# A fused attention and two-layer expert kernel on one core: cast and rest of a split issued one position apart, the output's low weights loaded by a transfer of their own, q and k loads spread over ten positions

## Chip, core and metric

The kernel runs on one core of one Trainium2 chip. The metric is the device time of one execution in microseconds (us). Before the change three runs gave 1924.92, 1928.77 and 1932.10 us; the median is 1928.77 us.

## What is computed

```
x   = softmax(q kT / 8) v            8 batches, 8 heads, 576 tokens, chunks of 64 tokens, head size 64
y1  = (silu(x  wg) * (x  wv)) wo     4608 tokens, 512 -> 1536 -> 512
xn  = y1 / sqrt(mean(y1^2) + 1e-6) * rms_g
out = (silu(xn wg2) * (xn wv2)) wo2  4608 tokens, 512 -> 1536 -> 512
```

Attention is local to a chunk of 64 tokens. The weights arrive as 64-bit floats; q, k and v as 32-bit floats.

## The kernel before, in words

**Numbers.** Every matrix product of the two layers is made of three matmuls: each operand is split into a high part (`hi`, a cast on ACT to the fp32r type) and a low part (the rest, a subtraction on DVE or POOL), and `mm3` (line 585) issues high x high, high x low and low x high. So a split is a chain: cast on ACT, subtraction on another engine, and often a store or a matmul behind it.

**First layer.** The first 3584 tokens go in 7 blocks of 512 (`j` = 0 to 6), each through 12 chunks of the hidden size (`f`), so 84 iterations (line 1346). PE's order in iteration n is: `emit_g` (12 matmuls), `emit_v` (12 matmuls), then `emit_y` of iteration n-1 (12 matmuls). The loop calls `run(0)` after `emit_g`, `run(1)` after `emit_v`, `run(2)` at the end: three **positions** an iteration, 36 a block. `put` hangs any other work on a position, and `spread` hands out a list of DMAs over several positions. Engines execute in program order, and all DMAs but a few at the very end are issued by one queue, SP's, also in program order.

**What hangs on positions.** In blocks 1 to 5: attention of the later tokens (tiles of 128 tokens, one each 6.75 positions, `score_at`): maximum and exponentials (`att_m`), the normalisation on POOL (`att_n`, line 480), DVE transposes (`att_td`, line 496), the DVE transposes of the next tile's q and k (`trans_att`, line 409); the loads of q, k and v by groups of five chunks of 64 tokens (`load_qk`, `load_v`, `issue`, line 398). A group inside one batch row needs 32 q and k transfers, a group over a batch's end 64. Then the second layer's weights: load (`load_w64`, line 109), two ACT steps (`rebase`), two DVE steps (`to_f32`), sums of blocks on POOL (`comb_add`), splits (`comb_split`, cast line 218, subtraction line 219, store line 220). Then sums of the first layer's own weights for its last 1024 tokens (`whole`, `first_add`, `first_keep`), at the places of `w1_at`. Then the root mean square of the block before (`rms_...`).

**Low weights.** The high parts of the first layer's weights stay in memory. The low parts don't fit: block 0 makes them (`to_lo`, line 164) and stores them to DRAM through the list `keep` (line 1288), and each later iteration loads its chunk (`load_lo`, line 184): one tile of 768 KB that holds the parts of gate, value and output, in three slots.

```
            if n + 2 < len(iters) and n + 2 >= NF:
                load_lo(*iters[n + 2])
...
            sg, product = emit_g(l, j, f)
            run(0)
...
            if prev is not None:
                emit_y(*prev)
```

The order of chunks turns round from block to block, so a block begins on the three chunks that the last one ended on and loads nine.

In block 0 `conv1` runs three times an iteration. Call c converts weight c, makes the low part of weight c-1 and issues the store of weight c-6; weights come in the order gate, value, output of each chunk.

**The rest.** From about 915 us the program works through six superblocks `s` of 7 products each (a Strassen form): superblock 0 is the first layer of the last 1024 tokens, 1 to 5 are the second layer. A superblock has 84 steps of 6 matmuls (gate and value), then 84 of 3 (output). Weights come through a ring of 16 slots (`load_ring`); in superblock 0 `ring_split` (lines 886 and 888) splits the sums of weights when they have landed. `late` and `norm` hang work on the steps of superblocks 0 and 1: the root mean square of block 6 and of the last 1024 tokens (`tail_...`), and the last four pairs of output weights (`late_o`).

Of the kernel before, what the change touches and what calls it, by code (L numbers as in the profile page):

```python
# [19 lines left out]
def tile_kernel(  # L20
# [19 lines left out]
    nc = tc.nc  # L40
# [129 lines left out]
    def slot(j, f):  # L170
        if f >= 3:
            return slot(j, f - 3)
        return f if j == 0 else slot(j - 1, NF - 1 - f)

    def low_of(l, j, f, nm):
        if j and f < 3:
            return low_of(l, j - 1, NF - 1 - f, nm)
        return wl_[l, j, f][:, "gvo".index(nm)]

    def load_lo(l, j, f):  # L180
        if f < 3:
            return
        t = wlo.tile([P, 3, KD * P], F32R, tag=f"l{slot(j, f)}", name=f"l_{l}_{j}_{f}")
        nc.sync.dma_start(out=t.bitcast(F32), in_=lo1_d[chunk(j, f)])
        wl_[l, j, f] = t

# [27 lines left out]
    def comb_split(nm, fp, k, w=None):  # L214
        t = comb[1, nm, fp][k]
        if w is None:
            w = cv.tile([P, 2, HK], F32R, tag="ws", bufs=4, name=f"ws{nm}{fp}_{k}")
        nc.scalar.copy(w[:, 0], t)
        nc.gpsimd.tensor_sub(w[:, 1], t, w[:, 0].bitcast(F32))
        nc.sync.dma_start(out=w2_d["gvo".index(nm), fp, :, k], in_=w.bitcast(F32))  # L220

    PLAIN = {"g": ((0, 0), (0, 1), (1, 1)), "v": ((0, 0), (0, 1), (1, 1)), "o": ((0, 0), (1, 0), (1, 1))}

    def whole(nm, j, p, side):
        f = 2 * p + side
        t = cv.tile([P, KD * P], F32, tag="wa", bufs=2, name=f"wa{nm}{f}")
# [446 lines left out]
    def rms_split(j):  # L673
        n = blocks[j][1]
        acc = rms[j]
        ah = st.tile([P, 512], F32R, tag="ah", name=f"ah{j}")
        al = st.tile([P, 512], F32R, tag="al", name=f"al{j}")
        nc.scalar.copy(ah[:, :n], acc[:, :n])
# [25 lines left out]

    def rms_newton(j):
        n = blocks[j][1]
        ms, r = rms[j]
        nc.gpsimd.tensor_mul(ms[:, :n], ms[:, :n], r[:, :n])
# [43 lines left out]
    for i in range(NW // P, NT_):  # L752
        j = order[i] * P // NW
        if i >= 8:
# [24 lines left out]
        for c in (2 * i, 2 * i + 1):  # L779
            g = where[c][0]  # L780
            if g > 0 and c == groups[g][-1] and g + 2 < len(groups):
                dq, dv, nq = {4: (21, 18, 10), 7: (3, 9, 12), 8: (8, 12, 12)}.get(i, (1, 9, 7))
                spread(0, 0, b + dq, nq, lambda g=g: load_qk(g + 2))
                spread(0, 0, b + dv, 3, lambda g=g: load_v(g + 2))
    for j in range(1, NB):
        pj = j - 1
        for d in range(KD):
            put(0, j, 3 + 2 * d, lambda pj=pj, d=d: rms_sq(pj, d))
        put(0, j, 14, lambda pj=pj: rms_split(pj))
        put(0, j, 17, lambda pj=pj: rms_mm(pj))  # L790
        for z in range(4):
            put(0, j, (22, 22, 24, 24)[z] if j == 1 else (20, 21, 23, 26)[z], lambda pj=pj, z=z: rms_rec(pj, z))
        put(0, j, 29 if j == 1 else 27, lambda pj=pj: rms_newton(pj))
        for d in range(KD):
            put(0, j, (30, 32, 33, 34)[d] if j == 1 else 28 + 2 * d, lambda pj=pj, d=d: rms_x(pj, d))
# [4 lines left out]
    for x, (nm, f) in enumerate(w2):  # L800
        pos = NP + 6 * x
        put(0, 0, pos, lambda nm=nm, f=f: load_w64(1, nm, f))
        put(0, 0, pos + 4, lambda nm=nm, f=f: rebase(1, nm, f))
        put(0, 0, pos + 5, lambda nm=nm, f=f: to_f32(1, nm, f))
        if f >= NP2:
            fp = f - NP2
            for d, what in enumerate((
                ((comb_add, 3), (comb_add, 4)),
                ((comb_split, 3), (comb_add, 5)),
                ((comb_split, 4), (comb_add, 6)),  # L810
                ((comb_split, 0), (comb_split, 5)),
                ((comb_split, 1), (comb_split, 6)),
                ((comb_split, 2),),
            )):
# [62 lines left out]
    wsn = 0  # L877

    def ring_split(n):
        nonlocal wsn  # L880
        while wsn < min(n, wnext, len(wseq)):
            s, m, fp, k = wseq[wsn]
            wsn += 1
            if s == 0 and k > 2:
                t = wt[s, m, fp, k]
                nc.scalar.copy(t[:, 0], t[:, 1].bitcast(F32))
                eng = nc.gpsimd if wsn > 36 and m != "g" else nc.vector
                eng.tensor_sub(t[:, 1], t[:, 1].bitcast(F32), t[:, 0].bitcast(F32))
# [659 lines left out]
```

## Time and profile before

| what | value |
|---|---|
| median of three runs | 1928.77 us |
| the profiled execution | 1927.03 us, span from first to last instruction 1924.9 us |
| busy share | PE 92%, DVE 67%, ACT 42%, POOL 29% |
| mean granted TensorE clock | 0.967 of full speed |
| chain that ended last | PE 55%, DMA 13%, DVE 12%, POOL 7% |

"Busy" of PE counts a matmul from its issue to its modelled end, so that a row's count of matmuls against its length says more than its busy time. PEclk is the granted clock as a share of full speed (1.0 is 2.4 GHz, 0.5 is 1.2 GHz). A wait in the views is idle time of an engine and what ended it.

### The profile page before, as it was taken

How to read it: one execution, taken by the hardware profiler on the slowest of the kernel's cores; microseconds unless marked ns; L12 is line 12 of the kernel's file. 1: busy time of each engine (PE TensorE's matmuls, PEld its weight loads, DVE VectorE, ACT ScalarE, POOL GpSimd, SP SyncE). 2: the span in 40 equal slices, each digit the busy share in tenths (PEclk: the TensorE clock that was granted, in tenths of full speed). 3: DMA queues.
4: the chain of work that ended last, by engine and by line, in shares of the span. 5: the costliest groups of instructions: out<-in, count | busy, mean ns of one | idle time of the engine just before them, and what ended most of it. 6: DMA issues, size and time to landing. Idle time of an engine off the chain costs nothing.

```text
span 1924.9 us, 29765 instructions
## 1 busy us (share of the span) xinstructions
PE 1765.0 (92%) x9978; PEld 1468.4 (76%) x9978; DVE 1293.9 (67%) x2242; ACT 813.9 (42%) x1902; POOL 567.1 (29%) x551
## 2 busy tenths in 40 slices
PE   7989798888849979899988988999999999999998
PEld 5768576676638757788867776788888888999998
DVE  7976376575646666846768956795578458659566
ACT  7753333333324434323545633352345335336243
POOL 1003345255446345522244673021011001102000
PEclk9999899899979989999999999999999999999999
DMA  9976666677557567535465466868767776887986
GB/s 240 301 184 159 178 170 165 183 202 187 178 151 205 172 188 221 177 99 192 120 227 165 135 197 224 257 208 245 215 186 224 237 210 202 270 279 252 299 253 171
DMA packets 461670, 391.04 MB, mean 203 GB/s; under 512 B 278480, under 2 KB 334544, under 8 KB 461520
## 3 DMA queue, kind: packets, MB, share of 16 engines
q1 hardware_dynamic: 459920, 388.96, 68.9%
q8 instruction: 80, 1.31, 0.3%
q14 instruction: 70, 0.57, 0.1%
q10 hardware_dynamic: 1600, 0.20, 0.1%
HBM read 309.07 MB, written 79.95 MB: 202 GB/s over the span
## 4 chain that ended last, share of the span: by engine, by line
PE 55%; DMA 13%; DVE 12%; POOL 7%; issue 6%; SPq 4%; ACT 3%; DVEq 0%; POOLq 0%; ACTq 0%
DMA lo_scratch<-l 3%; SPq L398 3%; DVE pT L496 3%; PE v L586 2%; DMA l<-lo_scratch 1%; PE g L586 1%; PE v L588 1%; PE v L587 1%; PE g L588 1%; PE g L587 1%; ACT p L452 1%; PE ygA L587 1%; PE yvA L588 1%; PE ygA L588 1%; PE yvA L586 1%
## 5 line engine op out<-in xcount | busy, mean ns | idle before, releaser
L1028 POOL TENSOR_TENSOR h<-h,h 128x512 f32<-128x512 f32 (+1 forms) x36 | 47.3, 1313 | 558.4 <-DVE h L1006 539.4
L586 PE MATMUL g<-xh,wg 128*128 128x512 f32 x336 | 139.0, 414 | 36.1 <-DVE sg L599 34.3
L496 DVE STREAM_TRANSPOSE pT<-p 32x128 f32<-32x128 f32 x448 | 135.6, 303 | 46.5 <-POOL p L480 40.3
L1064 DVE TENSOR_TENSOR hp<-h,hp 128x512 fp32r<-128x512 f32 (+1 forms) x216 | 149.7, 722 | 6.2 <-ACT hp L1063 5.9
L588 PE MATMUL g<-xh,l 128*128 128x512 f32 x336 | 136.5, 406 | 15.1 <-DMA l<-lo_scratch 15.1
L1063 ACT CAST hp<-h 128x512 fp32r<-128x512 f32 (+1 forms) x216 | 122.0, 584 | 58.1 <-PE yvA L588 21.9
L986 ACT ACTIVATE sig<-sgt 128x512 f32<-128x512 f32 (+1 forms) x108 | 64.5, 597 | 185.7 <-DVE sgt L994 185.5
L586 PE MATMUL v<-xh,wv 128*128 128x512 f32 x336 | 134.8, 401 | 7.3 <-DVE sg L615 4.6
L587 PE MATMUL g<-xl,wg 128*128 128x512 f32 x336 | 135.4, 403 | 0.3 <-DVE xl L580 0.3
L987 DVE TENSOR_TENSOR sgt<-sgt,sig 128x512 f32<-128x512 f32 (+1 forms) x108 | 71.7, 664 | 93.8 <-ACT sig L986 93.7
L588 PE MATMUL v<-xh,l 128*128 128x512 f32 x336 | 131.8, 392 | 0.0
L587 PE MATMUL v<-xl,wv 128*128 128x512 f32 x336 | 131.5, 391 | 0.0
L925 POOL TENSOR_TENSOR xf<-xf,xf 128x512 f32<-128x512 f32 (+1 forms) x48 | 79.6, 1659 | 156.7 <-DMA wro<-w_scratch 67.8
L618 ACT CAST hh<-sg 128x512 fp32r<-128x512 f32 x84 | 51.8, 617 | 143.5 <-DVE sg L615 143.5
L586 PEld LDWEIGHTS g<-xh,wg 128*128 128x128 f32 x336 | 66.0, 196 | 55.4 <-DVE sg L599 39.4
L480 POOL TENSOR_TENSOR p<-p,r 128x512 f32<-128x512 f32 x36 | 39.7, 1102 | 225.2 <-DVE r L479 181.4
L599 DVE SCALAR_TENSOR_TENSOR sg<-sg,g 128x512 f32<-128x512 f32 x84 | 57.0, 679 | 61.4 <-ACT sg L598 60.9
L587 PE MATMUL y<-hl,wo 128*128 128x512 f32 x168 | 69.7, 415 | 28.6 <-DVE hl L620 28.2
L588 PEld LDWEIGHTS g<-xh,l 128*128 128x128 f32 x336 | 65.9, 196 | 32.1 <-DMA l<-lo_scratch 17.2
L586 PE MATMUL y<-hh,wo 128*128 128x512 f32 x168 | 69.0, 411 | 20.5 <-ACT hh L618 20.5
L598 ACT ACTIVATE sg<-g 128x512 f32<-128x512 f32 x84 | 50.0, 596 | 89.3 <-PE g L588 89.2
L586 PEld LDWEIGHTS v<-xh,wv 128*128 128x128 f32 x336 | 63.7, 190 | 24.0 <-DVE sg L615 7.2
(860 smaller groups left out, 5362.2 us busy)
## 6 DMA issues: line engine op xcount, KB each, us to landing
wrg<-w_scratch SPq DMA_DIRECT2D x210, 256.0 KB, 3.6
wrv<-w_scratch SPq DMA_DIRECT2D x210, 256.0 KB, 3.4
wro<-w_scratch SPq DMA_DIRECT2D x210, 256.0 KB, 3.2
l<-lo_scratch SPq DMA_DIRECT2D x54, 768.0 KB, 4.9
w_scratch<-wsg SPq DMA_DIRECT2D x42, 256.0 KB, 3.3
w_scratch<-wsv SPq DMA_DIRECT2D x42, 256.0 KB, 2.9
w64g<-in_moe_w_gate_dram SPq DMA_DIRECT2D x19, 512.0 KB, 6.3
w64v<-in_moe_w_val_dram SPq DMA_DIRECT2D x19, 512.0 KB, 5.4
```

What stands on the lines that cost most here:

```text
L398: nc.sync.dma_start(out=o, in_=i)
L496: nc.vector.transpose(out=pT[o:o + 32, :, r:r + 32], in_=pt[r:r + 32, :, z, b * 32:b * 32 + 32])
L586: nc.tensor.matmul(o, sh, mh, start=first, stop=False, skip_group_check=free)
L587: nc.tensor.matmul(o, sh, ml, start=False, stop=False, skip_group_check=free)
L588: nc.tensor.matmul(o, sl, mh, start=False, stop=last, skip_group_check=free)
L599: return sg, lambda: nc.vector.scalar_tensor_tensor(out=sg[:, :n], in0=sg[:, :n], scalar=1.0, in1=g[:, :n], op0=ALU.add, op1=ALU.mult)
L618: nc.scalar.copy(hh[:, :n], sg[:, :n])
L925: nc.gpsimd.tensor_sub(o, a, b)
L986: nc.scalar.activation(sg[:, :tw], src[:, :tw], AF.Sigmoid)
L987: nc.vector.tensor_mul(t[:, :tw], src[:, :tw], sg[:, :tw])
L1063: nc.scalar.copy(hh[:, :tw], src)
L1064: nc.vector.tensor_sub(hl[:, :tw], src, hh[:, :tw].bitcast(F32))
```

## The change

Nothing is computed otherwise. Slots and transfers of the low weights change; nearly all else is the order in which the same instructions are issued.

Low weights: gate and value in tiles of 512 KB with three slots (`load_lo`), output in tiles of 256 KB with two slots of its own (`load_lo_o`, called after `emit_y`). In block 0 the output's low part is made straight into such a slot.

```
-            wl_[0, 0, f] = wlo.tile([P, 3, KD * P], F32R, tag=f"l{f % 3}", name=f"l_0_0_{f}")
-        lo = wl_[0, 0, f][:, z]
+            wl_[0, 0, f] = wlo.tile([P, 2, KD * P], F32R, tag=f"l{f % 3}", name=f"l_0_0_{f}")
+        if z == 2:
+            wl_[0, 0, f, "o"] = wlo.tile([P, KD * P], F32R, tag=f"lo{f % 2}", name=f"lo_0_0_{f}")
+        lo = wl_[0, 0, f, "o"] if z == 2 else wl_[0, 0, f][:, z]
...
-        nc.sync.dma_start(out=t.bitcast(F32), in_=lo1_d[chunk(j, f)])
+        nc.sync.dma_start(out=t.bitcast(F32), in_=lo1_d[chunk(j, f), :, 0:2])
...
+    def load_lo_o(l, j, f):
+        if f < 2:
+            return
+        t = wlo.tile([P, KD * P], F32R, tag=f"lo{slot(j, f, 2)}", name=f"lo_{l}_{j}_{f}")
+        nc.sync.dma_start(out=t.bitcast(F32), in_=lo1_d[chunk(j, f), :, 2])
...
             if prev is not None:
                 emit_y(*prev)
+            if NF <= n + 1 < len(iters):
+                load_lo_o(*iters[n + 1])
             v_product()
```

Splits in two steps: `comb_split` becomes `comb_cast` and `comb_rest`, `rms_split` and `tail_split` give their cast to `rms_cast` and `tail_cast`, and POOL's product goes from `rms_newton` and `tail_newton` to `rms_mul` and `tail_mul`.

```
+    COMB = (
+        (7, comb_add, 3), (7, comb_add, 4), (8, comb_add, 5), (8, comb_cast, 3), (8, comb_cast, 4),
+        (9, comb_rest, 3), (9, comb_rest, 4), (10, comb_add, 6), (10, comb_cast, 0), (10, comb_cast, 5),
+        (11, comb_rest, 0), (11, comb_rest, 5), (12, comb_cast, 1), (12, comb_cast, 6),
+        (13, comb_rest, 1), (13, comb_rest, 6), (13, comb_cast, 2), (14, comb_rest, 2),
+    )
...
-        put(0, 0, pos, lambda nm=nm, f=f: load_w64(1, nm, f))
+        put(0, 0, pos + 1, lambda nm=nm, f=f: load_w64(1, nm, f))
         put(0, 0, pos + 4, lambda nm=nm, f=f: rebase(1, nm, f))
-        put(0, 0, pos + 5, lambda nm=nm, f=f: to_f32(1, nm, f))
+        put(0, 0, pos + 6, lambda nm=nm, f=f: to_f32(1, nm, f))
```

Attention and its loads (`a` is the tile's `score_at`; `b` is `a` - 1):

```
-            put(0, 0, a + 2, lambda i=i: att_n(i))
-            put(0, 0, a + 3, lambda i=i: att_td(i, 0))
-            put(0, 0, a + 4, lambda i=i: att_td(i, 1))
             if i + 1 < NT_:
-                put(0, 0, a + 5, lambda i=i: trans_att(i + 1))
+                put(0, 0, a + 2, lambda i=i: trans_att(i + 1))
+            put(0, 0, a + 3, lambda i=i: att_n(i))
+            put(0, 0, a + 4, lambda i=i: att_td(i, 0))
+            put(0, 0, a + 5, lambda i=i: att_td(i, 1))
...
-                dq, dv, nq = {4: (21, 18, 10), 7: (3, 9, 12), 8: (8, 12, 12)}.get(i, (1, 9, 7))
+                dq, dv, nq = {4: (21, 18, 10), 7: (3, 9, 12), 8: (8, 12, 12)}.get(i, (1, 11, 10))
                 spread(0, 0, b + dq, nq, lambda g=g: load_qk(g + 2))
-                spread(0, 0, b + dv, 3, lambda g=g: load_v(g + 2))
+                spread(0, 0, b + dv, 4, lambda g=g: load_v(g + 2))
```

The root mean square: cast at position 13, subtraction at 14, reciprocals at 20, 21, 23, 25, POOL's product at 26, Newton step at 28, scaling at 29, 31, 32, 34. `whole` gets a third buffer; `w1_at` puts 3, 4, 4, 4, 3 pairs into blocks 1 to 5 in place of 3, 3, 6, 3, 3, and output pairs run one iteration later.

The ring: casts two steps ahead of the subtractions, both further ahead than before, and POOL subtracts for the value weights alone.

```
-                eng = nc.gpsimd if wsn > 36 and m != "g" else nc.vector
...
+            while wsn[z] < min(n + 2 - 2 * z, wnext, len(wseq)):
...
+                    eng = nc.gpsimd if wsn[z] > 36 and m == "v" else nc.vector
...
-                    ring_split(wn + 5)
+                    ring_split(wn + 7)
...
-                ring_split(wn + 6)
+                ring_split(wn + 8)
```

`late_o` is drawn out from 12 to 19 steps (load at 0, first step at 4 in place of 3, casts and rests one step apart) and begins at steps 28 and 48 of superblock 0 and 24 and 42 of superblock 1, in place of 30, 50, 3 and 23; the tail's squares begin at step 0, its cast stands at 9 and 17, its subtraction at 11 and 19, its product at 37 and 45, its Newton step at 39 and 47.

## Rows read from the trace of the kernel before

**Rows 1.** The page's first part: busy us, share of the span, instructions.

```profile
PE 1765.0 (92%) x9978; PEld 1468.4 (76%) x9978; DVE 1293.9 (67%) x2242; ACT 813.9 (42%) x1902; POOL 567.1 (29%) x551
```

**Rows 2.** Windows, undisturbed: length; busy (count) PE, PEld, DVE, ACT, POOL; PEclk; DMA share; GB/s.

```profile
584.40:592.59 8.19, 8.19 (x37) 6.76 (x36) 6.18 (x18) 3.34 (x9) 6.73 (x10) 1.00 0.82 227
574.93:584.40 9.47, 9.47 (x101) 7.70 (x100) 6.17 (x10) 5.81 (x24) 3.29 (x5) 1.00 0.34 83
...
1250.00:1650.00 400.00, 400.00 (x1767) 331.02 (x1766) 285.21 (x427) 171.53 (x302) 55.99 (x37) 1.00 0.74 216
```

**Rows 3.** Windows, blocks 0 to 5 of the first layer.

```profile
25.03:151.40 126.37, 113.72 (x725) 89.38 (x726) 103.55 (x169) 84.17 (x149) 6.93 (x5) 0.97 0.88 244
151.40:284.47 133.07, 115.82 (x788) 91.78 (x786) 80.03 (x167) 48.63 (x167) 49.10 (x53) 0.92 0.62 167
284.47:417.45 132.98, 115.21 (x755) 90.35 (x754) 84.69 (x176) 49.00 (x158) 60.66 (x66) 0.94 0.65 178
417.45:574.93 157.48, 113.76 (x755) 89.82 (x754) 88.03 (x176) 50.53 (x160) 77.05 (x82) 0.88 0.63 178
574.93:701.29 126.36, 110.25 (x819) 88.14 (x818) 82.30 (x172) 52.02 (x176) 57.38 (x63) 0.95 0.69 193
701.29:814.92 113.63, 107.62 (x755) 85.67 (x754) 84.57 (x173) 47.93 (x156) 65.08 (x69) 1.00 0.63 188
```

**Rows 4.** Windows, the four stretches of blocks 1 to 4 that lose most.

```profile
195.70:233.80 38.10, 25.47 (x140) 18.80 (x138) 11.81 (x28) 11.09 (x31) 11.90 (x15) 0.78 0.63 173
334.60:368.50 33.90, 23.95 (x140) 18.03 (x139) 14.66 (x31) 10.58 (x21) 13.17 (x16) 0.80 0.67 185
514.80:574.93 60.13, 29.76 (x173) 23.74 (x172) 24.24 (x48) 11.28 (x35) 21.10 (x23) 0.74 0.55 153
665.20:690.90 25.70, 10.98 (x38) 7.92 (x37) 8.38 (x19) 6.22 (x25) 5.92 (x6) 0.73 0.72 210
```

**Rows 5.** PE's waits, 151.4 to 815 us: us in total, times, longest.

```profile
PE g L586 <- DVE sg L599: 28.4, 8, 14.7
...
PE g L588 <- DMA l<-lo_scratch: 15.1, 4, 5.2
```

**Rows 6.** Timeline of SP, ACT and DVE in the last stretch: start, length, instruction, idle before.

```profile
676.17 4.01 SPq L398 DMA_DIRECT2D xk<-in_k_dram  x8
...
682.50 0.40 ACT L218 CAST wsv<-wtv 128x256 fp32r<-128x256 f32 x1 [6.62 <-DMA w_scratch<-wsv]
...
684.05 1.21 DVE L135 SCALAR_TENSOR_TENSOR cmv<-w64v,cmv 128x512 uint32<-128x512 uint32 x1 [15.37 <-ACT cmv L125]
```

**Rows 7.** SP's own waits, blocks 1 to 4.

```profile
SPq L184 <- PE y_b L588: 63.3, 17, 10.3
```

**Rows 8.** Line 398 in blocks 1 to 4: issue time in ns, least, median, most.

```profile
L398 SPq DMA_DIRECT2D xq<-in_q_dram x209: 311/444/1236, 151.2 to 700.7; - x105
```

**Rows 9.** DVE's waits, 151.4 to 815 us.

```profile
DVE r L479 <- ACT r L456: 47.1, 22, 3.6
...
DVE pT L496 <- POOL p L480: 39.7, 16, 15.2
```

**Rows 10.** DVE's longest wait in block 0, 25 to 151.4 us.

```profile
DVE l L164 <- DMA lo_scratch<-l: 17.0, 6, 6.9
```

**Rows 11.** DMA issues of the page's kind: count, KB each, median us to landing.

```profile
lo_scratch<-l SPq DMA_DIRECT2D x36, 256.0 KB, 4.5
```

**Rows 12.** Timeline of DVE, block 0, the output's low part of chunk 10.

```profile
130.04 0.69 DVE L164 TENSOR_TENSOR l<-cro,wo 128x512 fp32r<-128x512 f32 x1
```

**Rows 13.** Timeline of SP, block 0, the 27th of 36 stores: output of chunk 8.

```profile
133.90 0.34 SPq L1288 DMA_DIRECT2D lo_scratch<-l  x1
```

**Rows 14.** Window, most of superblock 0 and the start of superblock 1.

```profile
960.00:1210.00 250.00, 220.51 (x894) 173.05 (x893) 180.20 (x246) 117.97 (x247) 127.93 (x117) 0.95 0.61 194
```

**Rows 15.** Groups by line and shape: busy us, mean ns, idle before.

```profile
L888 POOL TENSOR_TENSOR wro<-wro 128x256 fp32r<-128x256 f32 x24 | 24.6, 1047 | 5.4 <-ACT wro L886 5.3
...
L888 DVE TENSOR_TENSOR wrg<-wrg 128x256 fp32r<-128x256 f32 x24 | 15.3, 643 | 3.4 <-ACT wrg L886 3.4
```

More of the change, by code (lines that the diff above doesn't have):

```diff
@@ L225, in whole @@
         f = 2 * p + side
-        t = cv.tile([P, KD * P], F32, tag="wa", bufs=2, name=f"wa{nm}{f}")
+        t = cv.tile([P, KD * P], F32, tag="wa", bufs=3, name=f"wa{nm}{f}")
         h = whi[0, nm, f]
@@ L676, in rms_split @@
         ah = st.tile([P, 512], F32R, tag="ah", name=f"ah{j}")
+        nc.scalar.copy(ah[:, :n], acc[:, :n])
+        rms[j] = (acc, ah)
+    def rms_split(j):
+        n = blocks[j][1]
+        acc, ah = rms[j]
         al = st.tile([P, 512], F32R, tag="al", name=f"al{j}")
-        nc.scalar.copy(ah[:, :n], acc[:, :n])
         nc.gpsimd.tensor_sub(al[:, :n], acc[:, :n], ah[:, :n].bitcast(F32))
@@ L703, in rms_rec, with rms_mul @@
         nc.vector.reciprocal(out=r[:, a], in_=r[:, a])
+    def rms_mul(j):
+        n = blocks[j][1]
+        ms, r = rms[j]
+        nc.gpsimd.tensor_mul(ms[:, :n], ms[:, :n], r[:, :n])
     def rms_newton(j):
@@ L1148, in tail_split @@
         nc.scalar.copy(both[:, 0], acc)
+        tail[z] = (acc, both)
+    def tail_split(z):
+        acc, both = tail[z]
         nc.gpsimd.tensor_sub(both[:, 1], acc, both[:, 0].bitcast(F32))
@@ L1221, in late_o, with rest, cast @@
         spl = {"n": 0}
-        def split(k):
+        def rest(k):
+            comb_rest("o", fp, k)
+        def cast(k):
             n = spl["n"]
@@ L1412, in tile_kernel @@
         pj = NB - 1
-        late = {4 + 2 * d: [lambda d=d: rms_sq(pj, d)] for d in range(KD)}
-        late[14] = [lambda: rms_split(pj)]
-        late[17] = [lambda: rms_mm(pj, True)]
-        for z in range(4):
-            late[20 + 2 * z] = [lambda z=z: rms_rec(pj, z)]
-        late[28] = [lambda: rms_newton(pj)]
-        for d in range(KD):
-            late[30 + 2 * d] = [lambda d=d: rms_x(pj, d)]
-        norm = {}
-        for fp in range(LATE, NP2):
-            first, z = divmod(fp - LATE, 2)
-            for d, fn in enumerate(late_o(fp)):
-                (norm if first else late).setdefault((3 if first else 30) + 20 * z + d, []).append(fn)
+        late, norm = {}, {}
@@ new lines, in when @@
+        def when(t, n, fn, *a):
+            t.setdefault(n, []).append(lambda: fn(*a))
+        for d in range(KD):
+            when(late, 4 + 2 * d, rms_sq, pj, d)
+            when(late, 32 + 2 * d, rms_x, pj, d)
+            when(late, 20 + 2 * d, rms_rec, pj, d)
+        when(late, 13, rms_cast, pj)
+        when(late, 14, rms_split, pj)
+        when(late, 17, rms_mm, pj, True)
+        when(late, 28, rms_mul, pj)
+        when(late, 30, rms_newton, pj)
+        for fp, (t, n) in zip(range(LATE, NP2), ((late, 28), (late, 48), (norm, 24), (norm, 42))):
+            for d, fn in late_o(fp).items():
+                when(t, n + d, fn)
@@ L1434, in tile_kernel @@
-            norm.setdefault(34 + 8 * z, []).append(lambda z=z: tail_newton(z))
-            for d in range(KD):
-                norm.setdefault(37 + 2 * d + 8 * z, []).append(lambda z=z, d=d: tail_x(z, d))
+                when(norm, 2 * d + 8 * z, tail_sq, z, d)
+                when(norm, 29 + 2 * d + 8 * z, tail_rec, z, d)
+                when(norm, 41 + 2 * d + 8 * z, tail_x, z, d)
+            when(norm, 9 + 8 * z, tail_cast, z)
+            when(norm, 11 + 8 * z, tail_split, z)
+            when(norm, 16 + 8 * z, tail_mm, z)
@@ L1437, in tile_kernel @@
+            when(norm, 27, tail_sqrt, z)
+            when(norm, 37 + 8 * z, tail_mul, z)
+            when(norm, 39 + 8 * z, tail_newton, z)
         extra = {0: late, 1: norm}
```

121 lines of the change are left out of this document (58 added, 63 removed), and 8 rows, old and new, of the table w1_at.

## The prediction

> **What bounds the kernel now.** I began with the busy shares: PE is busy 92% of the span [rows 1], so a gain can only come from time in which PE idles or goes slowly. How much that is, the undisturbed stretches say [rows 2]: an iteration of the first layer takes 8.19 us, one with an attention tile 9.47 (1.28 more), and late in the run 1767 matmuls take 400 us, 0.2264 us each.
>
> Next the windows by block [rows 3]. A block should take 12 x 8.19 = 98.3 us and 1.28 for each of its 5, 5.5 or 6 tiles, so 104.7 to 106. Blocks 1 to 5 take 133.1, 133.0, 157.5, 126.4 and 113.6: 27.8, 28.3, 52.8, 20.4 and 8.9 us too much, 138 in all. Four short stretches hold most of it [rows 4]: against 18.1, 18.1, 25.9 and 8.2 us for their iterations they lose 20.0, 15.8, 34.2 and 17.5, together 87.5 us; 50.5 us are strewn over the rest. In these stretches the granted clock is 0.73 to 0.80: after PE has idled, part of the next matmuls run at 1.2 GHz in place of 2.4, and that is inside the 87.5. The other loss is at the seam of the layers: from 960 to 1210 us 894 matmuls stand where 250 / 0.2264 = 1104 would, so 47.5 us [rows 14].
>
> Then the reason. PE's rows name DVE's evacuation (28.4 us in 8 waits) [rows 5], but DVE is not the source. In the fourth stretch [rows 6] SP spends 4.01 us on eight k transfers; behind these stands the store of a finished weight; ACT waits 6.62 us for that store's buffer; DVE waits 15.37 us for ACT; PE waits for both. All four stretches lie where a group of q and k over a batch's end is loaded: 64 issues in seven positions. At 0.444 to 0.50 us each [rows 8, 6] that is 28 to 32 us of SP in 7 x 2.94 = 20.6 us (a position is a third of 8.83, the mean of the two iterations). And SP comes to it late: at each iteration's head it stops at the load of the low weights until PE has read the slot's output part, at that iteration's end, 63.3 us in 17 waits [rows 7]. Everything behind it is up to one iteration late.
>
> **The change part by part.**
>
> *Output's low weights apart.* The gate and value tile is free when PE has finished `emit_v` of the iteration before, so the load at the iteration's head no longer stops SP. The added wait is at `load_lo_o`, in position 2, for the same end of `emit_y` (up to 10.3 us each [rows 7]). Behind it stand only the DMAs of that position and of the next two; they go out when PE ends the iteration. SP is then late by a third of an iteration, some 3 us, in place of up to 9. The loads get more room: the 15.1 us that PE waited for them [rows 5] should go. Ten more issues a block at about 0.4 us cost SP 4 us a block.
>
> *q and k over ten positions.* 32 us of issues now fall in 29.4. With the other issues (some 10 in seven positions, 18 in ten, at 0.4 us) SP falls behind by 11.4 + 4 = 15 us before and 2.6 + 7 = 10 after; with the lateness at the start 24 and 13. The mean loss of the four stretches, 87.5 / 4 = 22, is 2 us less than the 24, so I take 2 us as the lateness that is borne: 11 us a stretch remain, 44, a gain of **43**. Bounds: the whole 87.5; or 25, if SP starts as late as now and 62 remain. I take the middle because both causes are halved, neither removed. The transposes of q and k come three positions earlier and their loads end three later: 15.5 - 9 = 6.5 positions or 19 us are left, and 13 us of lateness still fit; if not, DVE waits for them, 0 to 5 us a stretch, which the range carries.
>
> *Chains one position apart.* In blocks 1 to 5 DVE waits 47.1 us for the exponentials' sums, 39.7 for POOL's product [rows 9]; one position between each step hides 2.94 us, and the mean of the first is 2.1. The weight's load has a position less before its first step, but no longer waits behind the low weights. With block 3's six pairs cut to four, I take 30 of the strewn 50.5 us; bounds 10 and 45.
>
> *The seam.* The same cure for the root mean square, the tail and `late_o`, which in superblock 1 no longer starts together with the tail's squares. I take 18 of the 47.5; bounds 0 and 30. The 24 output subtractions that go from POOL to DVE cost DVE at most 24 x 0.643 = 15.4 us and relieve POOL of 24.6 [rows 15]. I price the swap at nothing, between 15 lost and 9 won, because DVE's part need not lie on PE's path. *Beside that:* the Trainium skill ("SBUF — State Buffer", Who interferes with whom) says that a VectorE instruction with two SBUF inputs and a GpSimd instruction that reads SBUF shut each other out for a whole instruction. By that, POOL's 24.6 us would come off DVE's waiting and the swap would win 24.6 - 15.4 = 9 us, the time 1839 us; by the rows alone it stays at 1848, and no row here separates the two.
>
> *Two output slots in block 0.* This one costs. Call c of `conv1` issues the store of weight c-6. Before, the wait for a slot was gate's: it needs a store issued two calls earlier, and DVE waited 17.0 us in 6 waits [rows 10]. Now the output part of chunk f needs that of chunk f-2 stored, issued one call earlier. A store lands 4.5 us after its issue [rows 11], a call comes each 126.37 / 36 = 3.5 us. In the trace the output part of chunk 10 was written at 130.04 us [rows 12], 3.9 us before the store of chunk 8's was even issued [rows 13]. So DVE will wait there in most of ten chunks. DVE is 103.55 of 126.37 us busy in this block [rows 3] and has little room; behind the waiting subtraction stand the next weight's conversion and the hidden layer's low part, for which PE waits. The landing less a call is 1 us, SP's own lateness adds 1 to 3: against 10 waits of 2 to 4 us stand the 17.0 us of gate's, most of which go. I take **12 us lost**; bounds 0 (the same stores only move the wait) and 28 (nothing is saved elsewhere).
>
> *At no cost:* the third `whole` buffer, the moved reciprocals, scalings and POOL products, and the ring's earlier casts, whose weights have 16 - 9 = 7 steps of 6 x 0.2264 = 1.36 us, 9.5 us, from issue; if that cover were gone, ACT would wait once a step.
>
> **The sum.** 43 + 30 + 18 - 12 = 79 us. The profiled execution took 1927.0 us (span 1924.9 and 2.1 around it), 1.7 below the median of 1928.8. 1927 - 79 = **1848 us**.
>
> **The rivals.** A difference within 0.5%, 9.6 us, can hardly be told from none here.
>
> *SP stays the bound (0.22).* The same q and k issues and 60 more; if the backlog and not the start decides, the stretches give back 25 only, the strewn waits 10, the seam 5, and block 0 takes 12 to 28: 12 to 28 us won, 1899 to 1915; I write 1900. For it: SP's 32 us in 29.4 leave it nothing spare.
>
> *Almost all goes (0.12).* The backlog stays under what is borne: 75 + 40 + 25 - 8 = 132, 1795. For it: the iterations between the third and the fourth stretch that I took as undisturbed lose nothing with the same work on all engines [rows 2].
>
> *No difference (0.08).* SP's halt at the low weights was idle time without consequence, and the waits moved with their steps: gains of about 20 meet block 0's loss, 1919 to 1937.
>
> *Slower (0.08): block 0's two slots.* Each late chunk delays DVE, DVE delays the conversion that frees SP's next load, SP issues the next store later: the waits feed one another. The price: at 7 us a chunk 70, less the 17 saved, 53 lost against gains of 35: 1945. It decides from about 6 us a chunk, if the stretches give no more than their lower bound. Against it: while DVE waits, SP works off its own queue, so that the next store comes sooner.
>
> **How the numbers follow.** My forecast has 0.50. Its own range is 1814 (the stretches give 65, half way to their bound, and block 0 takes nothing) to 1882 (they give 25 and block 0 takes 28). The range of 8 in 10 takes in the near part of "almost all" and SP's case: 1798 to 1910; outside lie 0.16 of the last two and some 0.04 below. Faster by over 0.5%: 0.50 + 0.22 + 0.12 = 0.84; within: 0.08; slower: 0.08.
>
> **What will show it.** Right: SP's wait of `load_lo` for `emit_y` gone, one of `load_lo_o` in its place; PE's wait for low weights gone; the four stretches still there but of about 11 us each; block 3 near 125 us; block 0 longer, at 138 us, with DVE's wait for stores at the output part and over 25 us; over 960 matmuls from 960 to 1210 us of the old place. Wrong: a block 0 that has not grown, four stretches as long as now, or a new wait of DVE for q and k.

## The result and the profile after

The changed kernel takes 1812.34 us, the median of four runs (1807.24 to 1814.78), against 1927.45 us for four runs of the kernel before beside it: a ratio of 0.9397, 95% interval 0.9369 to 0.9425, or 115 us. The forecast was 1848 us with a range of 1798 to 1910, so the direction and the range held, and the gain was 36 us larger than forecast. The profiled execution took 1807.24 us, 5.1 us less than the median; its span is 1805.5 us, at a mean granted clock of 0.990 (0.967 before).

The page's first part, engine by engine (PE was 92% busy before [rows 1]):

```profile
PE 1735.9 (96%) x9978; PEld 1455.5 (81%) x9978; DVE 1289.7 (71%) x2266; ACT 811.7 (45%) x1902; POOL 549.1 (30%) x527
```

PE issues the same 9978 matmuls in 29 us less of busy time (they run less often at the lower clock) and idles 90 us less. The 24 subtractions that went from POOL to DVE stand in the counts.

Windows by block, blocks 0 to 5, columns as in [rows 2]:

```profile
26.00:153.40 127.40, 113.95 (x724) 89.51 (x725) 101.90 (x169) 84.04 (x149) 5.26 (x4) 0.97 0.89 246
153.40:270.30 116.90, 111.06 (x788) 89.00 (x787) 80.87 (x169) 49.94 (x169) 49.87 (x53) 0.97 0.69 189
270.30:386.90 116.60, 109.10 (x756) 87.07 (x755) 81.97 (x171) 48.17 (x157) 68.76 (x74) 0.99 0.77 216
386.90:498.50 111.60, 107.12 (x755) 87.26 (x754) 82.55 (x175) 48.46 (x157) 65.96 (x71) 0.98 0.76 210
498.50:613.20 114.70, 109.78 (x819) 88.21 (x818) 85.62 (x177) 51.81 (x173) 65.87 (x70) 0.99 0.79 226
613.20:721.50 108.30, 106.46 (x755) 86.34 (x754) 81.88 (x174) 49.42 (x162) 61.80 (x67) 1.00 0.78 227
```

Beside [rows 3]: block 0 grew by 1.1 us; blocks 1 to 5 went from 663.5 to 568.1 us, 95.4 less. By the prediction's measure of undisturbed blocks they should take 525.4, so 42.7 us are still lost. Block 3, which lost most, gained most: 45.9 us.

Windows, the four stretches over a batch's end where they lie now, and last the seam, 93.5 us earlier than in [rows 14] because all that lies ahead of it is so much shorter:

```profile
206.40:239.20 32.80, 28.87 (x173) 21.91 (x171) 18.66 (x40) 13.34 (x35) 8.50 (x11) 0.95 0.79 241
305.40:361.10 55.70, 48.20 (x319) 37.04 (x312) 34.66 (x74) 24.54 (x80) 22.16 (x26) 0.97 0.78 224
483.70:529.90 46.20, 38.61 (x273) 30.04 (x272) 27.25 (x58) 15.54 (x53) 18.07 (x20) 0.96 0.74 198
599.70:634.10 34.40, 30.76 (x237) 23.37 (x236) 22.81 (x48) 12.84 (x39) 18.61 (x20) 0.95 0.74 199
866.50:1116.50 250.00, 235.87 (x1010) 188.92 (x1009) 202.04 (x297) 124.53 (x258) 110.44 (x94) 0.99 0.69 221
```

The stretches hold 3, 5, 4 and 3 iterations with 1, 2, 2 and 2 tiles, the second also two matmuls of the root mean square. At 8.19 us an iteration, 1.28 a tile and 0.2264 such a matmul they lose 7.0, 11.7, 10.9 and 7.3 us, 36.9 in all, in place of 87.5 [rows 4], so 5.8 of the 42.7 are strewn over the rest, in place of 50.5. At the seam 1010 matmuls stand where 894 stood and 1104 would: a loss of 94 x 0.2264 = 21.3 us in place of 47.5.

Waits of PE and SP in blocks 1 to 5, and two of DVE's (us in total, times, longest):

```profile
PE y L607 <- ACT hh L639: 11.7, 6, 4.1
...
PE g L609 <- DMA l<-lo_scratch: 1.2, 1, 1.2
...
SPq L193 <- PE y_b L609: 13.9, 12, 2.8
...
DVE hl L641 <- ACT hh L639: 87.2, 34, 10.7
...
DVE pT L517 <- POOL p L501: 4.3, 6, 2.1
```

and the first of DVE's two in the same blocks before:

```profile
DVE hl L620 <- ACT hh L618: 2.7, 5, 0.7
```

PE's wait for low weights fell from 15.1 to 1.2 us [rows 5]. SP's 63.3 us for `emit_y` in four blocks [rows 7] are 13.9 in five now, at `load_lo_o` (line 193), none over 2.8. DVE's wait for POOL's product went from 39.7 to 4.3 us, and its 47.1 us for the exponentials' sums [rows 9] no longer stand in the list. Not all of DVE's idle time went, though: it now stands 87.2 us at the low part of the hidden layer, for ACT's cast `hh`, where it stood 2.7 before. The largest wait that PE has left is for the same cast; what makes that late comes at the end of the experiments.

### The profile page after: what moved, and what is told of

It is laid out like the page before. It is cut to its first block, busy times and chain, and to the rows that moved or that the text cites. A ratio compares the mean times of both kernels' runs of the same rounds, so it can differ in the third digit from the quotient of the medians.

```text
span 1805.5 us, 29839 instructions
## 1 busy us (share of the span) xinstructions
PE 1735.9 (96%) x9978; PEld 1455.5 (81%) x9978; DVE 1289.7 (71%) x2266; ACT 811.7 (45%) x1902; POOL 549.1 (30%) x527
## 4 chain that ended last, share of the span: by engine, by line
PE 67%; DVE 11%; DMA 8%; SPq 4%; POOL 3%; ACT 3%; issue 3%; DVEq 0%; ACTq 0%; POOLq 0%
SPq L419 3%; PE v L607 3%; PE v L608 2%; PE v L609 2%; PE g L607 2%; PE g L608 2%; PE g L609 2%; DMA lo_scratch<-lo 2%; PE ygA L608 1%; PE ygA L609 1%; PE ygA L607 1%; PE y L607 1%; PE yvA L609 1%; PE yvA L608 1%; PE yvA L607 1%
## 5 line engine op out<-in xcount | busy, mean ns | idle before, releaser
L517 DVE STREAM_TRANSPOSE pT<-p 32x128 f32<-32x128 f32 x448 | 135.5, 303 | 10.6 <-POOL p L501 4.3
L641 DVE TENSOR_TENSOR hl<-sg,hh 128x512 fp32r<-128x512 f32 x84 | 72.5, 863 | 90.6 <-ACT hh L639 90.3
L607 PE MATMUL g<-xh,wg 128*128 128x512 f32 x336 | 133.1, 396 | 3.8 <-DVE sg L620 2.1
L609 PE MATMUL g<-xh,l 128*128 128x512 f32 x336 | 131.2, 390 | 1.2 <-DMA l<-lo_scratch 1.2
L608 PE MATMUL g<-xl,wg 128*128 128x512 f32 x336 | 131.1, 390 | 0.4 <-DVE xl L601 0.4
L609 PE MATMUL v<-xh,l 128*128 128x512 f32 x336 | 131.3, 391 | 0.0
L607 PE MATMUL y<-hh,wo 128*128 128x512 f32 x168 | 69.2, 412 | 11.7 <-ACT hh L639 11.7
L1032 DVE TENSOR_TENSOR h<-h,sgt 128x512 f32<-128x512 f32 (+1 forms) x108 | 74.0, 685 | 3.7
L607 PEld LDWEIGHTS v<-xh,wv 128*128 128x128 f32 x336 | 63.3, 188 | 16.4 <-ACT wo L156 2.2
```

The costliest lines, as they stand in the source:

```text
L517: nc.vector.transpose(out=pT[o:o + 32, :, r:r + 32], in_=pt[r:r + 32, :, z, b * 32:b * 32 + 32])
L607: nc.tensor.matmul(o, sh, mh, start=first, stop=False, skip_group_check=free)
L608: nc.tensor.matmul(o, sh, ml, start=False, stop=False, skip_group_check=free)
L609: nc.tensor.matmul(o, sl, mh, start=False, stop=last, skip_group_check=free)
L641: return product, lambda: nc.vector.tensor_sub(hl[:, :n], sg[:, :n], hh[:, :n].bitcast(F32))
L1032: nc.vector.tensor_mul(h[:, :tw], src[:, :tw], sgt[pos][:, :tw])
```

## The experiments

Twelve kernels ran, four runs each, beside six or seven runs of the kernel before on the same chip. Where time went inside a kernel is read between the first matmuls of its blocks; "seam" is the time of the 1600 matmuls from the last iteration of the first layer's loop on. All are in us (to 0.1), and each comes from one profiled execution, except for the median. The ratios are to the runs of the kernel before that stand beside each kernel.

| kernel | median | ratio to before, 95% | block 0 | blocks 1-5 | block 3 | seam |
|---|---|---|---|---|---|---|
| before | 1927.45 | | 126.4 | 663.5 | 157.5 | 411.4 |
| changed | 1812.34 | 0.9369-0.9425 | 127.5 | 568.1 | 111.6 | 385.3 |
| only_low | 1906.50 | 0.9880-0.9928 | 129.8 | 640.6 | 149.9 | 409.1 |
| only_qk | 1900.05 | 0.9857-0.9898 | 124.1 | 639.9 | 151.2 | 408.5 |
| only_chains | 1898.70 | 0.9851-0.9895 | 125.4 | 637.6 | 152.5 | 408.1 |
| only_seam | 1901.29 | 0.9860-0.9913 | 122.5 | 665.1 | 161.0 | 385.8 |
| no_qk | 1825.23 | 0.9461-0.9501 | 128.8 | 584.4 | 117.6 | 386.2 |
| no_chains | 1858.50 | 0.9633-0.9679 | 133.3 | 614.1 | 145.4 | 385.4 |
| no_w1 | 1816.48 | 0.9404-0.9453 | 131.2 | 573.2 | 111.7 | 386.9 |
| no_low | 1859.11 | 0.9637-0.9683 | 122.8 | 623.3 | 149.1 | 385.9 |
| wa_two | 1829.64 | 0.9469-0.9521 | 129.6 | 589.5 | 131.3 | 386.0 |
| low_wa3 | 1880.75 | 0.9742-0.9787 | 130.2 | 615.2 | 122.2 | 411.7 |
| slots_pool | 1815.16 | 0.9401-0.9446 | 122.2 | 577.4 | 108.7 | 390.4 |
| aligned | 1761.64 | 0.9124-0.9167 | 121.4 | 529.1 | 105.0 | 386.6 |

### Each part alone

Four kernels add one part to the kernel before. `only_low` has the two tiles of low weights and `load_lo_o`, with two buffers of `whole` as before. `only_qk` is two lines:

```
-                dq, dv, nq = {4: (21, 18, 10), 7: (3, 9, 12), 8: (8, 12, 12)}.get(i, (1, 9, 7))
+                dq, dv, nq = {4: (21, 18, 10), 7: (3, 9, 12), 8: (8, 12, 12)}.get(i, (1, 11, 10))
...
-                spread(0, 0, b + dv, 3, lambda g=g: load_v(g + 2))
+                spread(0, 0, b + dv, 4, lambda g=g: load_v(g + 2))
```

`only_chains` has the new places of the attention, of `COMB` and of the root mean square, with the old `w1_at`. `only_seam` has the ring, `late_o` and the tail.

> The kernel before with one part of the change: the output's low weights in tiles and transfers of their own. Theory A (SP's lateness is the source: its halt at the low weights and the bursts of q and k loads): SP starts each burst on time, the four stretches of blocks 1 to 4 lose some 55 to 60 us in place of 87, the rest a few less; about 1890 us. Theory C (the steps of the chains, issued too close, are the source; SP's lateness is borne): within 8 us of the kernel before, 1920 us or more. Block 0 shows the price of two output slots in either: 0 to 12 us.

> The kernel before with one part: q and k loads over ten positions, v over four. Theory A: the burst's own backlog falls from 15 to 10 us, the lateness at its start stays; each of the four stretches gains some 5 us: about 1907 us. Theory C: within 8 us of the kernel before.

> The kernel before with one part: in blocks 1 to 6 the steps of attention, of the second layer's weights and of the root mean square one position apart. Theory A: the strewn waits of blocks 1 to 5 go (30 of 50 us), the four stretches stay: about 1897 us. Theory C: the stretches go as well, 60 to 95 us in all: 1835 to 1867 us.

> The kernel before with one part: the ring's earlier casts, the output's subtractions on DVE, and the new places of late output weights and of the root mean square in superblocks 0 and 1. Both theories: blocks 0 to 6 as before, and the 26 us that the seam gave in the changed kernel: about 1901 us.

Against 1923.94 us for the kernel before, they gave 17.4, 23.9, 25.2 and 22.7 us. The seam came out as expected, and it is independent: 385.8 us, as in the whole change. `only_low` lies between the two expectations, `only_qk` gave 7 us more than theory A had, and `only_chains` lies where theory A had it. Of these three each gave something, and each left block 3 at 149.9 us or more. Together the four give 89 of 115 us. So either the parts help each other, or a part that was in none of them holds the missing 26.

### Each part taken back

Four kernels take one part out of the changed kernel: `no_qk` (the two lines above, reversed), `no_chains`, `no_w1` (the old `w1_at`) and `no_low`. `no_chains` and `no_low` also got the old list and two buffers, so each of them takes three things out at once. Of the lists the lines of block 3 are shown, new and old:

```
...
-        (3, 5, "g"), (3, 4, "o"), (3, 2, "v"), (3, 1, "v"),
...
+        (3, 0, "v"), (3, 1, "v"), (3, 2, "v"), (3, 3, "v"), (3, 4, "v"), (3, 5, "v"),
...
```

> The changed kernel, with q and k loaded over seven positions again. Alone this part gave 24 us, and the four parts tried alone give 89 of the 115 that the whole gives. Theory A (lateness of SP is what PE waits for, and a stretch is cured only when all the lateness in it falls under what the buffers bear): taking one cure away brings back more than it gave alone, 35 to 50 us, 1847 to 1862 us, and the four stretches again lose 10 to 20 us each. Rival B (the parts are independent, and the missing 26 us are the new places of the whole weights' pairs, which were in none of the four): 24 us, 1836. Rival C (the other cures leave SP enough room for the dense loading): under 10 us, 1820.

> The changed kernel, with the chains of the attention, of the second layer's weights and of the root mean square in their old places. Alone this part gave 25 us. Theory A: 35 to 50 us, 1847 to 1862 us, with DVE's waits for the exponentials' sums (10.6 us in the changed kernel, 46.5 before) back above 30. Rival B (independent): 25 us, 1837. Rival C (SP is what matters, and the chains only fill time in which PE waits for SP anyway): under 10 us, 1820.

> The changed kernel, with the whole weights' pairs of the second superblock in their old places (six in the last half of the blocks 3, three in blocks 1, 2, 4 and 5). Theory B (the parts are independent and this place list is the missing fifth): 26 us, 1838, most of it in block 3, which takes 130 us or more against 111.6. Theory A (the gains add up to more because the lateness is shared, and the pairs are one more share of it): 5 to 20 us, 1817 to 1832, block 3 at 115 to 125. Rival C (the list has no part in it): 1812, block 3 at 112.

> The changed kernel, with the low weights again in one transfer of three parts at the head of an iteration, and with that the old places of the whole weights' pairs and their two buffers, since the new places need the apart transfers. Alone the apart transfer gave 17 us. Theory A: 17 us and the pairs' share and more, 45 to 60 us, 1857 to 1872; SP waits again about 60 us for the output part's reader, and PE waits again some 15 us for the low weights. Rival B (independent parts): 17 us and what the run with the old places alone loses, some 43 at the most, 1829 to 1855. Rival C (with the other cures SP's halt at the head costs nothing): the loss of the run with the old places alone and under 8 us more.

`no_qk` lost 12.9 us, half of what the part gave alone, so theory A, by which taking one cure away costs more than it gave, failed there. `no_w1` lost 4.1, and the intervals of the two ratios overlap: the list isn't the missing part either. `no_chains` and `no_low` lost 46 and 47 and fitted A, but with block 3 back at 145 to 149, and the two share something else: two buffers of `whole`. One expectation of `no_low` failed: SP's wait for `emit_y` in blocks 1 to 5 came back (93.2 us in 24 waits), but PE waited only 2.5 us for low weights there, not 15, so it isn't the apart transfer alone that ended that wait. (DVE's wait for the exponentials' sums is back in `no_chains`, 48.3 us in 23 waits. The 10.6 and 46.5 us that its expectation puts beside it were the idle time ahead of DVE's transposes.) The timeline of `no_chains` shows what two buffers do. SP, POOL, DVE and PE in block 3, start, length, instruction, idle before:

```profile
517.83 1.56 POOL L273 TENSOR_TENSOR wav<-wav,wav 128x256 f32<-128x256 f32 x2
...
525.72 2.36 SPq L423 DMA_DIRECT2D xq<-in_q_dram  x5
528.13 0.43 SPq L423 DMA_DIRECT2D xk<-in_k_dram  x1
...
530.22 0.38 SPq L276 DMA_DIRECT2D w_scratch<-wav  x1
...
534.60 1.26 POOL L253 TENSOR_TENSOR wav<-wv,l 128x512 f32<-128x512 f32 x1 [15.21 <-DMA w_scratch<-wav]
...
536.50 1.04 POOL L505 TENSOR_TENSOR p<-p,r 128x512 f32<-128x512 f32 x1
...
537.58 2.51 DVE L521 STREAM_TRANSPOSE pT<-p 32x128 f32<-32x128 f32 x8 [16.38 <-POOL p L505]
...
542.43 0.80 PE L612 MATMUL y<-hl,wo 128*128 128x512 f32 x1 [14.46 <-DVE hl L645]
```

POOL finished the sums of a pair of whole weights at 519.4 us. The store of the half that goes out first was issued at 530.2: SP issued without a pause until then, 6.4 of the 10.8 us q and k. With two buffers POOL's next sum waited 15.2 us for that store, and behind it on POOL stood the attention's product, for which DVE waited 16.4 us; behind DVE's transposes stood the low part that PE needs, and PE waited 14.5. One late store of a weight that nobody needs yet stops three engines.

### The third buffer

`wa_two` is `no_w1` with one number changed; `low_wa3` is `only_low` with the opposite change.

```
-        t = cv.tile([P, KD * P], F32, tag="wa", bufs=3, name=f"wa{nm}{f}")
+        t = cv.tile([P, KD * P], F32, tag="wa", bufs=2, name=f"wa{nm}{f}")
```

> The kernel of the run no_w1 (the changed kernel with the whole weights' pairs in their old places, 1816) with two buffers for these weights in place of three. New theory D (the third buffer is the missing term: POOL waits for the store of the weight two before, 31 to 46 us in up to 8 waits in every run with two buffers and 0.7 to 8 in the runs with three, and behind POOL stand the attention's products, DVE and PE): 1840 to 1855 us, most of it in block 3 (130 to 145 us against 111.7), POOL's waits for these stores above 25 us. Theory A (the low weights and the chains each cost over 35 us to take away for their own sake): under 1822 us, block 3 below 116. If D holds, the low split and the chains are worth only the rest of 1859 and 1858 less this time.

> The kernel before, with the output's low weights apart (as in the run only_low, 1906.5 us) and a third buffer for the whole weights in the room that this frees; nothing else of the change. Theory D: POOL's waits for its stores fall from 34.7 us in 4 waits to under 10, and block 3 from 149.9 us to 125 to 135: 1882 to 1890 us. Theory A (the buffer counts only when all the other lateness is gone): within 5 us of only_low, 1902 to 1910.

`low_wa3` takes 1880.75 us, 25.8 less than `only_low` (the ratios' intervals are apart: 0.9742 to 0.9787 against 0.9880 to 0.9928), and block 3 falls from 149.9 to 122.2. The two ran beside different runs of the kernel before (1927.09 and 1923.94 us); by the gains over these, 46.3 and 17.4, the buffer is worth 28.9. That is the size of the missing 26: the five parts tried alone add up to 115 or 118 us, where the whole change gives 115.1 (the intervals leave each term some 5 us, and the parts overlap, as the next paragraphs show, so that the sum fits this well is chance). POOL's waits for these stores, first `only_low`, then `low_wa3`:

```profile
POOL wav L253 <- DMA w_scratch<-wav: 34.7, 4, 13.5
POOL wav L253 <- issue: 18.0, 3, 14.4
```

```profile
POOL wav L253 <- DMA w_scratch<-wav: 19.5, 4, 11.8
```

The wait halved rather than fell under 10, since SP's stores still come late there. In the other direction `wa_two` loses 13.2 us against `no_w1`, less than the 23 to 39 expected, with block 3 at 131.3 in place of 111.7 and POOL's wait up from 8.2 to 32.0, first `no_w1`, then `wa_two`:

```profile
POOL wav L249 <- DMA w_scratch<-wav: 8.2, 4, 3.1
```

```profile
POOL wav L249 <- DMA w_scratch<-wav: 32.0, 6, 9.8
```

So theory D holds, with a smaller price where the other cures are in. With `wa_two` as the base, which has the same list and buffers, the chains are worth 1858.5 - 1829.6 = 28.9 us and the apart transfer 1859.1 - 1829.6 = 29.5.

### Block 0's slots and POOL's subtractions

`slots_pool` is the changed kernel with a third slot for the output's low weights, two buffers of `whole` to make room for it, and the ring's subtractions for the output weights back on POOL:

```
-            wl_[0, 0, f, "o"] = wlo.tile([P, KD * P], F32R, tag=f"lo{f % 2}", name=f"lo_0_0_{f}")
+            wl_[0, 0, f, "o"] = wlo.tile([P, KD * P], F32R, tag=f"lo{f % 3}", name=f"lo_0_0_{f}")
...
-        t = wlo.tile([P, KD * P], F32R, tag=f"lo{slot(j, f, 2)}", name=f"lo_{l}_{j}_{f}")
+        t = wlo.tile([P, KD * P], F32R, tag=f"lo{slot(j, f, 3)}", name=f"lo_{l}_{j}_{f}")
...
-        t = cv.tile([P, KD * P], F32, tag="wa", bufs=3, name=f"wa{nm}{f}")
+        t = cv.tile([P, KD * P], F32, tag="wa", bufs=2, name=f"wa{nm}{f}")
...
-                    eng = nc.gpsimd if wsn[z] > 36 and m == "v" else nc.vector
+                    eng = nc.gpsimd if wsn[z] > 36 and m != "g" else nc.vector
```

> The changed kernel with two edits at places apart: three slots for the output's low parts in place of two (and, for the room, two whole buffers, with the new list of pairs), read in block 0; and the output parts' 24 subtractions of the ring back on POOL, read in the seam from block 6's end over 1600 matmuls. Block 0: if the two slots cost the 12 us forecast, 115 us in place of 127.5; if the store waits only moved from the gate part to the output part, as DVE's 14.1 us for stores in the changed kernel against 17.0 before say, 124 to 130 us. Seam: by the Trainium skill (SBUF - State Buffer, Who interferes with whom) POOL's subtractions would shut DVE out for 24.6 us and the seam gets some 9 us longer than 385.3; by the rows, which show no wait of PE for either, it stays within 3 us. Blocks 1 to 5: by theory D 15 to 30 us more than the 568 of the changed kernel; if the new list needs no third buffer, under 5.

Block 0 and the seam, windows of `slots_pool`, and under them DVE's wait for a store in its block 0:

```profile
25.50:147.70 122.20, 113.17 (x724) 89.66 (x725) 102.59 (x169) 83.78 (x149) 5.27 (x4) 0.96 0.87 243
817.60:1208.00 390.40, 372.67 (x1602) 300.42 (x1601) 318.16 (x435) 192.96 (x384) 161.59 (x138) 0.99 0.65 201
```

```profile
DVE l L166 <- DMA lo_scratch<-l: 6.8, 2, 3.7
```

A third slot took 5.3 us off block 0, neither the 12 forecast nor nothing. The table agrees on the size: block 0 takes 127.5 to 133.3 us in seven of the eight kernels with two output slots (mean 130.1), 122.2 to 126.4 in the six others (mean 123.9). The eighth, `aligned` at 121.4, also loads q and k otherwise. So the price is 5 to 6 us, and the two ranges don't meet.

The seam took 390.4 us, against 385.3 to 386.9 in the eight kernels that have the new ring and leave these subtractions to DVE (mean 386.0): 4.4 us more with POOL, in one trace. So the swap won some 4 us of the seam's 26. The reason stands in DVE's rows. The seam of the changed kernel, and two of DVE's groups in it, first in the changed kernel, then in `slots_pool`:

```profile
813.90:1199.20 385.30, 370.67 (x1601) 299.47 (x1601) 312.60 (x459) 192.81 (x384) 140.01 (x114) 1.00 0.66 204
```

```profile
L1090 DVE TENSOR_TENSOR hp<-h,hp 128x512 fp32r<-128x512 f32 x72 | 52.1, 752 | 1.0 <-ACT hp L1089 1.0
...
L1092 DVE TENSOR_TENSOR h<-t,h 128x512 f32<-128x512 f32 x12 | 8.2, 682 | 0.0
```

```profile
L1090 DVE TENSOR_TENSOR hp<-h,hp 128x512 fp32r<-128x512 f32 x72 | 58.1, 837 | 1.6 <-ACT hp L1089 1.6
...
L1092 DVE TENSOR_TENSOR h<-t,h 128x512 f32<-128x512 f32 x12 | 11.5, 954 | 0.0
```

With POOL subtracting, DVE has 24 instructions fewer and is busy 5.6 us longer, because the same instructions take longer. Of DVE's 128x512 subtractions in `slots_pool`'s seam (lines 947 and 1070 to 1094), the 92 with no POOL instruction beside them take 0.70 us at most, the 29 that overlap one of POOL's 24 subtractions 1.22 us at the median. The rule of the Trainium skill that the prediction cites ("SBUF — State Buffer", Who interferes with whom) has DVE and POOL shut each other out in such pairs: these rows agree with it. Of the 9 us that the prediction worked out by it, 4.4 came; that DVE's added time is what PE waited for isn't shown.

Blocks 1 to 5 lost 9.3 us with two buffers and the new list, between the two expectations. The third slot works there too (SP's wait of 13.9 us for `emit_y` is 1.0), so the 9.3 us are net of what that gave. So the new list and the third buffer cure the same thing: beside either one the other is worth 5 to 9 us, and without both blocks 1 to 5 take 21.4 us more (`wa_two`).

### Groups of q and k cut at the batches' ends

What is left in the changed kernel lies where a group spans two batches and needs two transfers for each tile. The chain in the third stretch is that of [rows 6], one link shorter: SP's store is late, ACT waits for the store's buffer, its cast `hh` stands behind that, and DVE and PE wait for the cast. SP, then ACT, DVE and PE of the changed kernel:

```profile
489.80 0.87 SPq L234 DMA_DIRECT2D w_scratch<-wsv  x2
...
492.49 0.40 ACT L228 CAST wsv<-crv 128x256 fp32r<-128x256 f32 x1 [8.86 <-DMA w_scratch<-wsv]
492.80 0.61 ACT L639 CAST hh<-sg 128x512 fp32r<-128x512 f32 x1
...
493.45 0.80 DVE L641 TENSOR_TENSOR hl<-sg,hh 128x512 fp32r<-128x512 f32 x1 [10.41 <-ACT hh L639]
493.47 0.50 PE L607 MATMUL y<-hh,wo 128*128 128x512 f32 x1 [4.14 <-ACT hh L639]
```

`aligned` cuts the groups at the ends, four or five chunks each, so that one transfer fills a tile:

```
-        groups.append(list(range(c0, min(c0 + 5, NCH))))
+        n = 4 if c0 % (2 * SC) == 0 else 5
+        groups.append(list(range(c0, min(c0 + n, (c0 // SC + 1) * SC))))
...
-                dq, dv, nq = {4: (21, 18, 10), 7: (3, 9, 12), 8: (8, 12, 12)}.get(i, (1, 11, 10))
+                dq, dv, nq = {4: (21, 18, 10), 7: (-1, 9, 10)}.get(i, (1, 11, 10))
```

> The changed kernel with the groups of q and k cut at the batches' ends, so that no group needs two transfers a tile: 416 issues in place of 544, at most 32 in ten positions. If the 37 us that the stretches over a batch's end still lose are SP's issues: 20 to 35 us less, 1777 to 1792 us, and these stretches under 3 us each. If they are the other work of these iterations (weights' chains on ACT, DVE and POOL): within 8 us of 1812, with the losses at the same iterations.

It takes 1761.64 us, 50.7 less than the changed kernel and more than expected (43.9 between the profiled executions, of which 39.0 in blocks 1 to 5 and 6.1 in block 0); the ratio to the kernel before is 0.9146 (0.9124 to 0.9167). Its blocks 1 to 5:

```profile
147.10:253.60 106.50, 106.21 (x788) 86.86 (x787) 80.88 (x168) 49.90 (x169) 50.55 (x53) 1.00 0.79 209
253.60:358.60 105.00, 105.00 (x755) 86.17 (x754) 82.39 (x170) 48.17 (x157) 68.78 (x74) 1.00 0.85 237
358.60:463.60 105.00, 105.00 (x755) 86.19 (x754) 87.21 (x179) 50.00 (x160) 66.28 (x71) 1.00 0.86 243
463.60:571.20 107.60, 106.67 (x819) 87.31 (x818) 85.80 (x170) 52.29 (x177) 65.26 (x70) 1.00 0.88 242
571.20:676.20 105.00, 105.00 (x755) 86.17 (x754) 81.18 (x172) 48.55 (x158) 61.49 (x67) 1.00 0.73 217
```

In three blocks PE never stops and the clock stays at 1.00; the 104.7 us that the prediction worked out for an undisturbed block are reached within 0.3. The same bytes of q and k go through in less time, and in the changed kernel's stretches the DMA engines were busy for a share of 0.74 to 0.79 (up to 0.88 here), so the stretches were not short of bandwidth: what they lacked was SP's time. This version beats both kernels. It also moves the loads of two groups (the list's special places), and block 0 took 121.4 us in it; which of the 6 us there are owed to that wasn't tried apart.

## Why the prediction was right, and where its terms were off

**What bounds the kernel.** Shown right for blocks 1 to 5, with one addition. PE's idle time there came from SP's lateness: SP's halt at the head, its bursts and what waited behind them each gave time when cured alone, and with half the issues in a burst next to nothing is left of it (PE's waits in these blocks are 100.3 us before, 24.4 in the changed kernel, 1.2 in `aligned`). SP's wait for `emit_y` in these blocks, before and in `only_low`:

```profile
SPq L184 <- PE y_b L588: 84.7, 24, 10.3
```

```profile
SPq L193 <- PE y_b L613: 23.5, 8, 8.3
```

The addition: `only_chains` gave 25.2 us with this wait at 90.1 us, so the chains were a source of their own.

**The stretches (43 forecast).** Measured 50.6. The reason was right: 36.9 us remain in four stretches where 44 were to remain. Taking the middle between the bounds was near. But undoing the spread costs only 12.9 us, so this term was not the spread's and the apart transfer's alone: the chains and the buffer took their part in block 3, where the third stretch lies (131.3 us in `wa_two`, 145.4 in `no_chains`, 111.7 in `no_w1`).

**The strewn waits (30 forecast, 45 the upper bound).** Measured 50.5 - 5.8 = 44.7. Here the prediction named a wrong cause for part of it. It set "the third `whole` buffer" under "at no cost" and credited the pairs of block 3 that were cut from six to four; the runs give 4 us for that list, where the buffer is in, and 13 to 29 for the buffer. Block 3, forecast near 125, took 111.6. The row that says so was in the trace of before, among POOL's waits in blocks 1 to 5, which the prediction did not read:

```profile
POOL wav L228 <- DMA w_scratch<-wav: 43.4, 5, 16.0
```

The prediction saw the last link of that chain, DVE's 39.7 us for POOL's product [rows 9], and put all of it down to a chain issued too close. That was some half of it: this wait is 23.7 us in `only_chains`, and the buffer alone takes it from 44.6 (`only_low`) to 25.2 us (`low_wa3`).

**The seam (18 forecast).** Measured 26, and 22.7 by `only_seam`. Within the bounds; the swap, priced at nothing, is 4 of it. Which of the rest is owed to the ring's earlier casts, to `late_o` and to the tail wasn't tried apart, so the cause given for this term is argued and not shown.

**Block 0 (12 lost).** Measured 1.1 in the two traces, 5 to 6 over all kernels: 1.1 is luck, the longest of the six blocks without the price beside the shortest of the seven with it. The wait came where it was foretold, at the output's low part, but in the changed kernel it is 14.1 us in 7 waits for stores, 2.0 each, not over 25; with the same slots `no_chains` has the most:

```profile
DVE lo L166 <- DMA lo_scratch<-lo: 14.1, 7, 3.6
DVE lo L166 <- PE v L609: 6.7, 1, 6.7
```

```profile
DVE lo L166 <- DMA lo_scratch<-lo: 23.8, 8, 7.4
```

The gate's 17.0 us [rows 10] went, and these came in their place: mostly the lower bound's reason, "the same stores only move the wait". The size was off, not the step from DVE's wait to PE's time, though "DVE has little room" was read off a busy share of 82%, without a row that shows PE waiting. DVE's idle time before its low parts, all reasons together, is 21.5 to 23.8 us in the seven kernels whose block 0 takes 127.5 us or more, and 6.8 to 17.0 in the seven where it takes 126.4 or less; `aligned`, with 14.2 us and two slots, is one of the latter. With two slots, then, the wait is some 7 us longer in the mean (22.3 us in the seven, 15.2 in the five kernels with one tile of low weights), and the block some 6.

**The sum.** 95.4 + 26.1 - 1.1 for block 0 and - 1.0 at the start and the end make the 119.4 us between the spans; the forecast was 79. Of the 40 between, 22 are blocks 1 to 5, 8 the seam, 11 block 0. The 1812 us lie just outside the forecast's own range (1814 to 1882), and nearer to the 1795 of "almost all goes" than to 1848. Of the rivals, "SP stays the bound" fell: the apart transfer and the spread did lower SP's lateness. "Almost all goes" came nearer than its chance of 0.12 said for the strewn waits and the seam, not for the stretches. The slower case fell with its mechanism: DVE's waits for stores at the output part are at most 3.6 us long in the changed kernel and 7.4 in any with two slots, and never more than 23.8 in all, where the case needed 6 to 7 a chunk in ten chunks.

## What to carry to other kernels

Where one queue issues everything, count issues and not bytes: a group that straddles a border in DRAM doubles its issues, and cutting it at the border can be worth more than any spreading. Before a wait is put down to steps issued too close, follow it one engine further back: a store that is late behind other issues holds its buffer, and one more buffer at that place cut 13 to 29 us here. Price a part both ways, added to the old kernel and taken out of the new one, and look at what the kernels with the same loss have in common.

## What was not expected of the hardware

An issue on SP's queue costs nearly the same for a transfer of 8 KB as for one of 40. On the q and k loads of blocks 1 to 4 the median is 441 and 448 ns in the changed kernel, and 457 and 458 ns in `aligned`, with 314 issues in place of 404. In the whole run 144 of the changed kernel's 272 q loads carry 8 to 24 KB, and 192 of the 208 of `aligned` 32 or 40. Over the changed kernel's q loads the median rises from 426 ns at 8 KB through 439 at 24 to 458 at 40. So a smaller transfer bought hardly any time, and 404 x 0.445 - 314 x 0.457 = 36 us of the queue came free, where it was late.

A stall costs PE more than the time it stands: the mean granted clock is 0.967 before, 0.990 in the changed kernel and 0.996 in `aligned`, and PE's busy time for the same 9978 matmuls falls from 1765 to 1736 to 1719 us. Of the 46 us by which busy time fell in all, none is work that was removed.
